# Attention and two feed-forward layers on one core: a PSUM tile for each bank, float64 weights converted two pieces at a time, the end of attention planned with the first weights

## The chip, the cores and the metric

The kernel runs on one core of a Trainium2 chip. The metric is the device time of one execution in microseconds. TensorE (PE), VectorE (DVE), ScalarE (ACT), GpSimd (POOL) and SyncE (SP) each work through a queue of their own in order; SP issues nearly all transfers. Matrix products accumulate in PSUM, which has eight banks of 512 fp32 columns in each of 128 partitions.

## The reference

```python
def _attn_ref(q, k, v, cap):                       # 2 x 12 heads x 448 x 64
    scores = cap * np.tanh(scale * np.matmul(q, k.transpose(0, 1, 3, 2)) / cap)
    scores = scores - np.max(scores, axis=-1, keepdims=True)
    attn = np.exp(scores)
    attn = attn / (np.sum(attn, axis=-1, keepdims=True) + 1e-09)
    return np.matmul(attn, v)
...
x = attn_out.transpose(0, 2, 1, 3).reshape(896, 768)
h = x @ moe_w_in                                   # 768 x 2048, float64
x = np.where(h > 0.0, h, np.exp(np.minimum(h, 0.0)) - 1.0) @ moe_w_out
h = np.maximum(x @ moe2_w_in, 0.0)
return (h * h @ moe2_w_out).astype(np.float32)
```

The four weight matrices arrive as float64 and are turned into fp32 on the core. Each fp32 operand is split in a high and a low part (`xh`, `xl`), and a product is three matmuls: high by high, high by low, low by high.

## The kernel before, in words

Attention goes through twelve pairs of heads, `pairs[n]`, in an order written out by hand. The end of a pair is a chain: `pv_out` copies the result out of PSUM (`pvs`, ACT), a transfer brings the row of sums (`den`), DVE takes the reciprocal (`rd`, in `norm`), two more transfers spread it over the partitions (`far`, `bc`), and `norm_x` multiplies (`xn`) and splits into `xh` and `xl`. The first two column blocks of layer 1 (`First`, accumulated in `begun`) are multiplied while the last pairs finish; their sixth input chunk, `kc` = 5 with batch 1, needs the last pair.

From there on a planner (`Plan`) takes tasks with costs and the keys that they read and write, walks through them in time, and so sets each engine's order; PE's order is that of the tasks. In the planner's keys each PSUM bank is separate. The weights come in 93 pieces of 512 columns. A piece is loaded into one of five `raw` buffers, converted by three steps on ACT and two on DVE into one of three `f` buffers (L777 to L785), for a Strassen quad widened by three subtractions (L798, L804), and split into two of the `og` tiles (L811, L812, L817). Four or five pieces can wait there or be in use.

Each layer has four phases of 512 hidden columns. A phase computes two quads, (phase, 0) and (phase, 1), of 256 hidden columns each, and multiplies them with the output weights. A plain quad is 72 matmuls; a Strassen quad has seven terms, in the order 1, 5, 6, 2, 7, 3, 4, of nine matmuls each, 63. Terms 1, 6, 7, 4 run up in bank X, which is copied out in between (L926 on ACT or L927 on DVE), term 2 in bank Z, to which DVE adds an earlier copy (`plus`, L933), terms 5 and 3 in bank Y. The Strassen terms need sums of the inputs (`sums`, tiles `yh` and `yl`). In layer 1 the quads after the first two are Strassen, in layer 2 those after the first, 13 in all. The output of layer 2 is made token tile by token tile, in one bank each (`out2_side`, `out2_main`, matmuls at L1050), and DVE adds a finished bank to the result (L1086; in the first phase a copy, by ACT at L1080 or DVE).

PSUM is four tiles of two banks each:

```python
units = begun + [pacc.tile([P, 2, W], F32, name=f"acc{i}") for i in range(2)]
...
ux, uy = units[2 * s], units[2 * s + 1]
X, Z, Y = ((ux[:, 0, :S], ("bank", 2 * s, 0)), (ux[:, 1, :S], ("bank", 2 * s, 1)),
           (uy[:, 0, :S], ("bank", 2 * s + 1, 0)))
```

The framework that turns the program into instructions sets the semaphore waits from the tiles that an instruction touches and the order of the program.

Of the kernel before, what the change touches and what calls it, by code (L numbers as in the profile page):

```python
# [29 lines left out]
def attention_moe_kernel(  # L30
# [238 lines left out]
    def split_p(n, i, copy=nc.vector.tensor_copy):  # L269
        if n < 0:  # L270
            return
# [6 lines left out]
        copy(h, e)  # L278
        nc.vector.tensor_tensor(l, e, h.bitcast(F32), op=ALU.subtract)
# [27 lines left out]
    def pv_out(n, copy=nc.scalar.copy):  # L307
        if n < 0:
            return
        pvs = ap_.tile([P, 2, S], F32, name="pvs", tag="pvs", bufs=3)  # L310
        copy(pvs, st["po", n][:, :, :S])
        st["pvs", n] = pvs
        den = ap_.tile([D, 2 * S // D], F32, name="den", tag="den")
        nc.sync.dma_start(den, pvs[D:D + 1].rearrange("p h s -> p (h s)"))
        st["den", n] = den

    def norm(n):


        if n < 0:  # L320
            return
        den = st["den", n]
        rd = ap_.tile([D, 2 * S // D], F32, name="rd", tag="rd")
        nc.vector.reciprocal(rd, den)
        far = dp.tile([D, 2 * S // D], F32, name="far", tag="far")
        nc.sync.dma_start(far, rd)
        bc = ap_.tile([D, 2, S], F32, name="bc", tag="bc")
        flat = far.rearrange("p s -> (p s)").unsqueeze(0)
        nc.sync.dma_start(bc.rearrange("p h s -> p (h s)"), flat.to_broadcast([D, 2 * S]))
        st["bc", n] = bc  # L330
# [22 lines left out]
    class First:  # L353


        def __init__(self):
            self.loaded, self.done = 0, 0
            self.alone = False
            self.rest = lambda: None
# [10 lines left out]
        def f(self, i):  # L370
            return fs[i % 2][:, :3]

        def load(self, dma=nc.sync.dma_start):
            i = self.loaded
            self.loaded += 1
            if i < self.COUNT:
                m, k = divmod(i, 2)
                dma(raws[i][:, :3], rows(w_in1, 3 * k, 3, m * P, P))

        def words(self, i):  # L380
            return words(raws[i][:, :3])
# [31 lines left out]
        def settle(self):  # L413
            last, self.rest = self.rest, lambda: None
            last()

# [66 lines left out]
    def dve(n, fast=False):  # L483
        return 0.12 + n / (1920 if fast else 960)

    def act(n):
        return 0.2 + n / 1200
# [3 lines left out]
    class Plan:  # L491
# [7 lines left out]
        def add(self, options, reads=(), writes=(), lag=None):  # L499
# [16 lines left out]
            self.tasks.append((options, before, self.LAG if lag is None else lag))  # L516

        def run(self, free):
# [66 lines left out]
            for _, _, _, _, fn in self.order:  # L585
                fn()

# [5 lines left out]
    def early(i):  # L593
        for to, src in in_loads(w_in1, 1, i):
            nc.sync.dma_start(to(raws[RAWS[i]]), src)
# [4 lines left out]
    with tc.manual_schedule():  # L600
# [36 lines left out]
        for n in range(np_):  # L637
# [27 lines left out]
            elif n < 4 + EARLY and n > 3:  # L665
                early(n - 4)
# [25 lines left out]
        late_kc = 2 * (KC - 1)  # L692
        norm(np_ - 2)
        emit(first.advance())
        split_p(np_ - 1, 1)
        mm_in(0, begun[0], kb[6::2])
        pv(np_ - 1, 1)
        pv_out(np_ - 1)
        emit(norm_x(np_ - 3))
        emit(first.advance())  # L700
        mm_in(0, begun[0], kb[1:7:2])
        x, x_high, x_low = norm_x(np_ - 2)
        x()
        first.settle()
        norm(np_ - 1)
        mm_in(1, begun[1], kb[0::2])
        x_high()
        x_low()
        mm_in(0, begun[0], kb[7:late_kc:2])
        mm_in(1, begun[1], kb[1:late_kc:2])  # L710
        x, x_high, x_low = norm_x(np_ - 1, nc.scalar.copy)
        x()
        x_high()
        x_low()
        attn.close()
        pacc = ctx.enter_context(tc.tile_pool(name="pacc", bufs=1, space=PSUM))
        gp = ctx.enter_context(tc.tile_pool(name="gp", bufs=1))
        units = begun + [pacc.tile([P, 2, W], F32, name=f"acc{i}") for i in range(2)]
        raws.append(gp.tile([P, 4, P], I64, name="raw4"))
        fs.append(gp.tile([P, 8, P], F32, name="f2"))  # L720
        groups += [gp.tile([P, 7, P], F32R, name=f"og{i}") for i in range(4, 8)]
        yh, yl = (gp.tile([P, 4, KH, S], F32R, name=x) for x in ("yh", "yl"))
        gh, gl = (gp.tile([P, PF, NT], F32R, name=x) for x in ("gh", "gl"))
        eps = [gp.tile([P, 2, S], F32, name=f"ep{i}") for i in range(4)]
        yp = gp.tile([P, KC, NT], F32, name="yp")
        yt = yp.rearrange("p c n -> p (c n)").rearrange("p (t d) -> p t d", d=DM)

        plan = Plan()
        add = plan.add
        counts = {"piece": 0, "ep": 0, "set": 1}  # L730
        slots = list(OGS)
# [13 lines left out]
        def piece(loads, full):  # L745

            i = counts["piece"]
            counts["piece"] += 1
            r, k, s = RAWS[i % 5], FS[i % 3], slots.pop(0)
            slots.append(s)  # L750
            raw, f = raws[r], fs[k]
            kr, ka, kx = ("raw", r), ("f", k), ("fx", k)
# [3 lines left out]
            else:  # L756
                h, l = (z[:, 1, :KH].rearrange("p c n -> p (c n)")[:, :7 * P].rearrange(
                    "p (a n) -> p a n", n=P) for z in (xh, xl))
                kh, kl = ([(("x", kc, 1), z) for kc in range(KH)] for z in "hl")

            def load():
                for to, src in loads:
                    nc.sync.dma_start(to(raw), src)

            if i >= EARLY:
                add((SP, 2.9, load), writes=[kr], lag=1.5)
            lo, hi = words(raw)
            a = f[:, :4]
            if i % VMOD in VSET:
# [406 lines left out]
```

## Time and profile before

| what | value |
|---|---|
| median of 3 runs | 626.05 us (625.68 to 626.82) |
| the profiled execution | 627.81 us |
| span of its profile | 626.0 us |
| mean granted TensorE clock | 0.986 |
| PE, DVE, ACT busy | 93%, 81%, 68% of the span |
| matmuls | 2945 |

Rows of the trace give times in us from the start of the span. A row of the timeline has the start, the duration, the engine, the line, the operation, what it writes and reads, and in brackets how long the engine was idle before it and what ended that. A matmul's end is modelled; consecutive matmuls overlap, so the pace is read from start to start.

### The profile page before, as it was taken

The numbers are of one execution on the slowest core, as the hardware profiler recorded it, in microseconds if no ns is written. First come the engines' busy times: TensorE is split into PE (matmuls) and PEld (weight loads), VectorE is DVE, ScalarE is ACT, GpSimd is POOL, SyncE is SP. The second block draws the span as 40 slices with busy tenths as digits, with TensorE's granted clock in tenths as the row PEclk, the third lists the DMA queues.
The fourth block names the chain that finished last, engine by engine and source line by source line (L and its number), as shares of the span: only waits on it lengthen the run. The fifth ranks groups of instructions, "written<-read, shape, count | busy, mean of one in ns | idle before, by whom it ended". The sixth has DMA issues, their size and how long they took to land.

```text
span 626.0 us, 8153 instructions
## 1 busy us (share of the span) xinstructions
PE 579.6 (93%) x2945; PEld 496.0 (79%) x2945; DVE 504.6 (81%) x818; ACT 424.7 (68%) x575; POOL 17.2 (3%) x30
## 2 busy tenths in 40 slices
PE   8899999989999999999999997998999999999996
PEld 8676777768997799889888996886788778877884
DVE  4599999869898889789878899786688868877823
ACT  5799899638997896787668857774675467546400
POOL 3111011000000000000000000000000000000000
PEclk9899999997999999999999998999999999999999
DMA  5646641117433344224414423143234323321013
GB/s 126 159 99 153 146 106 46 35 55 228 126 112 102 99 138 142 93 102 134 135 34 147 124 68 100 45 160 101 69 111 129 97 68 129 121 88 34 1 60 117
DMA packets 70280, 64.71 MB, mean 103 GB/s; under 512 B 38240, under 2 KB 52960, under 8 KB 70240
## 3 DMA queue, kind: packets, MB, share of 16 engines
q1 hardware_dynamic: 68736, 63.57, 34.4%
q10 hardware_dynamic: 1504, 0.62, 0.4%
q8 instruction: 23, 0.38, 0.3%
q14 instruction: 17, 0.14, 0.1%
HBM read 61.34 MB, written 2.80 MB: 102 GB/s over the span
## 4 chain that ended last, share of the span: by engine, by line
PE 80%; DVE 7%; DMA 4%; ACT 4%; issue 2%; SPq 2%; POOL 0%; ACTq 0%; DVEq 0%; POOLq 0%
PE acc L1050 19%; PE acc L474 18%; PE acc L476 17%; PE acc L475 17%; PE po L302 6%; PE sc L250 3%; DMA qz<-in_q_dram 2%; DVE yp L1086 1%; DVE acc L933 1%; PE pt L183 1%; ACT e L259 1%; DVE ep L927 1%; SPq L133 1%; DVE xn L342 1%; DMA raw<-in_moe_w_in_dram 1%
## 5 line engine op out<-in xcount | busy, mean ns | idle before, releaser
L1050 PE MATMUL acc<-og,gh 128*128 128x512 f32 (+1 forms) x350 | 87.9, 342 | 8.2 <-DVE yp L1086 5.5
L779 ACT ACTIVATE f<-raw 128x512 f16<-128x512 f32 x93 | 73.3, 788 | 21.1 <-DVE f L785 15.5
L811 ACT CAST og<-f 128x512 fp32r<-128x512 f32 (+1 forms) x57 | 43.1, 763 | 60.1 <-DVE f L804 25.1
L1050 PEld LDWEIGHTS acc<-og,gh 128*128 128x128 f32 x350 | 59.7, 190 | 18.7 <-DVE yp L1086 8.0
L474 PE MATMUL acc<-xh,og 128*128 128x448 f32 x165 | 62.8, 381 | 11.2 <-DVE ep L927 4.3
L781 ACT ACTIVATE f<-raw 128x512 uint16<-128x512 uint8 x93 | 72.2, 778 | 0.0
L817 DVE TENSOR_TENSOR og<-f,og 128x512 fp32r<-128x512 f32 (+1 forms) x76 | 64.3, 850 | 5.2 <-ACT og L811 3.9
L785 DVE SCALAR_TENSOR_TENSOR f<-f 128x512 uint32<-128x512 uint32 x93 | 63.9, 688 | 5.0 <-ACT f L781 1.7
L777 ACT ACTIVATE f<-raw 128x512 f32<-128x512 f32 x93 | 60.5, 658 | 2.9 <-DVE og L817 2.4
L475 PE MATMUL acc<-xl,og 128*128 128x448 f32 x165 | 61.5, 373 | 0.2 <-DVE xl L349 0.2
L476 PE MATMUL acc<-xh,og 128*128 128x448 f32 x165 | 61.4, 372 | 0.0
L1050 PE MATMUL acc<-og,gl 128*128 128x512 f32 (+1 forms) x175 | 59.2, 338 | 0.0
L475 PE MATMUL acc<-gl,og 128*128 128x448 f32 x160 | 58.6, 366 | 0.0
L476 PE MATMUL acc<-gh,og 128*128 128x448 f32 x160 | 58.6, 366 | 0.0
L474 PE MATMUL acc<-gh,og 128*128 128x448 f32 x160 | 58.6, 366 | 0.0
L474 PE MATMUL acc<-yh,og 128*128 128x448 f32 x124 | 47.4, 382 | 9.1 <-DVE acc L933 7.3
L475 PE MATMUL acc<-yl,og 128*128 128x448 f32 x124 | 46.3, 373 | 2.1 <-DVE yl L862 2.1
L259 ACT ACTIVATE e<-sc,tsc 128x896 f32<-128x896 f32 (+1 forms) x48 | 43.4, 911 | 4.7 <-PE sc L250 4.7
L474 PEld LDWEIGHTS acc<-xh,og 128*128 128x128 f32 x165 | 31.6, 192 | 18.7 <-DVE ep L927 6.6
L476 PE MATMUL acc<-yh,og 128*128 128x448 f32 x124 | 46.2, 372 | 0.0
L1086 DVE TENSOR_TENSOR yp<-yp,acc 128x512 f32<-128x512 f32 (+1 forms) x33 | 21.6, 661 | 27.5 <-PE acc L1050 27.2
L783 DVE TENSOR_SCALAR f<-f 128x512 f32<-128x512 f32 x93 | 39.1, 421 | 2.8 <-ACT f L777 2.2
(145 smaller groups left out, 1280.4 us busy)
## 6 DMA issues: line engine op xcount, KB each, us to landing
raw<-in_moe_w_in_dram SPq DMA_DIRECT2D x45, 512.0 KB, 4.0
raw<-in_moe_w_out_dram SPq DMA_DIRECT2D x48, 256.0 KB, 3.9
raw<-in_moe_w_out_dram SPq DMA_DIRECT2D x24, 512.0 KB, 3.7
bc<-far SPq DMA_DIRECT2D x12, 224.0 KB, 3.3
k<-in_k_dram SPq DMA_DIRECT2D x15, 128.0 KB, 2.9
q<-in_q_dram SPq DMA_DIRECT2D x15, 128.0 KB, 2.8
v<-in_v_dram SPq DMA_DIRECT2D x15, 128.0 KB, 3.4
out_dram<-yp SPq DMA_DIRECT2D x7, 256.0 KB, 2.0
```

Of the source, the lines that this page charges most:

```text
L259: nc.scalar.activation(st["e", n][:, 2 * c:2 * c + w], st["sc", n, c][:, :w, :S], AF.Tanh, scale=tsc)
L474: nc.tensor.matmul(acc, w[0], x[0], start=first, stop=False, skip_group_check=True)
L475: nc.tensor.matmul(acc, w[0], x[1], start=False, stop=False, skip_group_check=True)
L476: nc.tensor.matmul(acc, w[1], x[0], start=False, stop=last, skip_group_check=True)
L777: add((ACT, act(512), lambda: nc.scalar.activation(a, hi.bitcast(F32), AF.Abs, scale=2.0 ** 16)), [kr], [ka])
L779: add((ACT, act(512), lambda: nc.scalar.activation(top, hi.bitcast(F32), AF.Copy, scale=2.0 ** -100)), [kr], [kx])
L781: add((ACT, act(512), lambda: nc.scalar.activation(bottom, last, AF.Copy, scale=1 / 32, bias=-31 / 64)), [kr], [kx])
L783: add((DVE, dve(512, True), lambda: nc.vector.tensor_scalar(a, a, 2.0, 2.0 ** 16 * CLAMP, op0=ALU.max, op1=ALU.min)), [ka], [ka])
L785: add((DVE, dve(512), lambda: nc.vector.scalar_tensor_tensor(out=b, in0=b, scalar=3, in1=q.bitcast(U32), op0=ALU.logical_shift_left, op1=A ...
L811: (ACT, act(n * P), lambda: nc.scalar.copy(h[:, :n], src)),
L817: (DVE, dve(n * P), lambda: nc.vector.tensor_tensor(l[:, :n], src, h[:, :n].bitcast(F32), op=ALU.subtract)),
L1050: nc.tensor.matmul(acc, x[:, f, g], w, start=a, stop=z, skip_group_check=True)
```

## The change

PSUM after attention becomes eight tiles of one bank each (`bank(i)`), four in the place of `psc` and four in the place of `ps1`. An instruction that read or wrote two banks becomes two (`halves` in `evac`, `out_add`). In a Strassen quad the copy of X after term 7 and the add that followed become one add. Weights are loaded and converted as couples of two pieces, in two `raw` and two `f` buffers of two pieces each; the split into `og` remains by piece. The quad (1, 0) of layer 1 and (0, 1) of layer 2 become plain. The end of attention, the last parts of `First` and the first third of the quad (0, 1) are put into a plan of their own, run before the SBUF of attention is given back. Couple 1 is loaded into the `raw` buffer that `First` gives back, ahead of the last `den` in SP's queue.

```diff
-    raws = [wp.tile([P, 4, P], I64, name=f"raw{i}") for i in range(4)]
-    fs = [wp.tile([P, 8, P], F32, name=f"f{i}") for i in range(2)]
+    raws = [wp.tile([P, 2, 4, P], I64, name=f"raw{i}") for i in range(2)]
+    fs = [wp.tile([P, 2, 8, P], F32, name="f0")]
...
+        def bank(i, n=S):
+
+            if banks[i] is None:
+                old, side, four = (scp, "left", range(4)) if i < 4 else (ps1x, "right", range(4, 8))
+                old.close()
+                pool = ctx.enter_context(tc.tile_pool(name=f"bank{side}", bufs=1, space=PSUM, side=side))
+                for k in four:
+                    banks[k] = pool.tile([P, W], F32, name=f"acc{k}")
+            return banks[i][:, :n]
...
+            raw, f = raws[k % 2], fs[(k + 1) % 2]
+            n = len(couples[k])
...
+            e = 512 * n
+            b = a.bitcast(U32)
+            add((ACT, act(e) + 0.04 * n, lambda: nc.scalar.activation(a, hi, AF.Abs, scale=2.0 ** 16)), kr, ka)
+            add((ACT, act(e) + 0.17 * n, lambda: nc.scalar.activation(
+                top, hi, AF.Copy, scale=2.0 ** -100)), kr, kx)
+            add((ACT, act(e) + 0.17 * n, lambda: nc.scalar.activation(
+                bottom, byte, AF.Copy, scale=1 / 32, bias=-31 / 64)), kr, kx)
+            add((DVE, dve(e, True), lambda: nc.vector.tensor_scalar(
+                a, a, 2.0, 2.0 ** 16 * CLAMP, op0=ALU.max, op1=ALU.min)), ka, ka)
+            add((DVE, dve(e), lambda: nc.vector.scalar_tensor_tensor(
+                out=b, in0=b, scalar=3, in1=q.bitcast(U32),
+                op0=ALU.logical_shift_left, op1=ALU.bitwise_or)), ka + kx, ka)
...
-                add((ACT, act(n), lambda: nc.scalar.activation(t, h, AF.Relu, scale=-1.0)), hk, tk)
+                    halves(ACT, act(S), lambda a, h: nc.scalar.activation(a, h, AF.Relu, scale=-1.0))
...
-            ux, uy = units[2 * s], units[2 * s + 1]
-            X, Z, Y = ((ux[:, 0, :S], ("bank", 2 * s, 0)), (ux[:, 1, :S], ("bank", 2 * s, 1)),
-                       (uy[:, 0, :S], ("bank", 2 * s + 1, 0)))
+            X, Z, Y = range(4 * s, 4 * s + 3)
...
-                7: (X, 3, lambda j: y(2, j), False, (c, ck, 0)),
+                7: (X, 3, lambda j: y(2, j), False, None),
...
+                if p == 7:
+                    plus(part(c, ck, 0), in_x, part(d, dk, 1))
...
-                        (DVE, dve(NT), lambda to=to, u=u: nc.vector.tensor_tensor(to, to, u, op=ALU.add)),
-                        keys + [("yp", m)], [("yp", m)],
-                    )
+                for b in range(B):
+                    at = 4 * s + 2 * i + b
+                    out_add(ph, gpart(yp, m, b), lambda at=at: bank(at), [("bank", at)], [("yp", m, b)], S)
...
+        end, before = np_ - 1, np_ - 2
+        norm_tasks(before)
+        first_tasks(2)
...
+        norm_x_tasks(before)
+        norm_tasks(end)
+        for kc in range(KC):
+            begun_product(1, kc, 0)
...
+        norm_x_tasks(end)
+        s1 = next_set()
+        made = [piece() for _ in range(KH - 1)]
+        plain_products(s1, range(1), made)
+        to_fp32()
+        free = plan.run({PE: 3.1, DVE: 2.1, ACT: 0.3, SP: 0.0})
+        attn.close()
```

How PE's rows change inside the Strassen quad (1, 1) of layer 1, with the semaphores that a row waits for, named by the engine that raises them. Before, the tile of banks X and Z is `acc`, that of bank Y too; the rows are the end of term 2 (`xh`, `xl`, into Z) and the start of term 7 (`yh`, `yl`, into X), with `og_77` to `og_80` and a part of `xh` as the weights:

```order
L476 MATMUL acc<-xh,og_78 128x448
L474 MATMUL acc<-xh 128x448
L475 MATMUL acc<-xl,xh 128x448
L476 MATMUL acc<-xh,xl 128x448
L474 MATMUL acc<-xh,og_79 128x448 [waits Activation_49]
L475 MATMUL acc<-xl,og_79 128x448
L476 MATMUL acc<-xh,og_80 128x448
L474 MATMUL acc<-yh,og_77 128x448
L475 MATMUL acc<-yl,og_77 128x448
L476 MATMUL acc<-yh,og_78 128x448
L474 MATMUL acc<-yh,xh 128x448 [waits DVE_49]
```

In the changed kernel bank X is `acc_1614`, Z `acc_1615` and Y `acc_1616`. The same place, from the last matmul of term 6 over term 2 to the first of term 7:

```order
L475 MATMUL acc_1614<-yh,og_75 128x448
L473 MATMUL acc_1615<-xh,og_1346 128x448
L474 MATMUL acc_1615<-xl,og_1346 128x448
L475 MATMUL acc_1615<-xh,og_1347 128x448
L473 MATMUL acc_1615<-xh,og_1348 128x448
L474 MATMUL acc_1615<-xl,og_1348 128x448
L475 MATMUL acc_1615<-xh,og_1349 128x448
L473 MATMUL acc_1615<-xh,og_74 128x448
L474 MATMUL acc_1615<-xl,og_74 128x448
L475 MATMUL acc_1615<-xh,og_75 128x448
L473 MATMUL acc_1614<-yh,og_1346 128x448 [waits DVE_49]
```

The wait inside term 2 is gone, and the wait at the start of term 7 is on another instruction: the copy of X that follows term 6, nine matmuls earlier.

ACT's rows at the end of attention, before; `e` is the last pair's scores, `f_75` and `f_76` belong to `First`, `f_1462` is the first converted piece of the planned weights, `raw_71` its float64 source:

```order
L259 ACTIVATE e<-sc,tsc 128x448 [waits PE_49]
L267 ACTIVATE e<-e,capt 128x1344 [waits Activation_49]
L409 CAST og_79<-f_75 128x384 [waits DVE_49]
L311 COPY pvs<-po 128x896 [waits DMAHW1_49,PE_49]
L409 CAST og_80<-f_76 128x384 [waits DVE_49]
L348 CAST xh<-xn 128x448 [waits DVE_49]
L779 ACTIVATE f_1462<-raw_71 128x512 [waits DMAHW3_49,DMAHW4_49,DMAHW2_49,DMAHW5_49,DMAHW1_49,DMAHW6_49,DMAHW0_49,DMAHW7_49,DVE_49,Pool_49]
L777 ACTIVATE f_1462<-raw_71 128x512
L781 ACTIVATE f_1462<-raw_71 128x512
L779 ACTIVATE f_75<-raw_72 128x512
```

And now, where `f_1345` and `raw_71` are the first couple, `f_73` and `raw_72` first the last parts of `First` and then the second couple:

```order
L261 ACTIVATE e<-sc,tsc 128x448 [waits PE_49]
L269 ACTIVATE e<-e,capt 128x1344 [waits Activation_49]
L806 ACTIVATE f_1345<-raw_71 128x2x512 [waits DMAHW5_49,DMAHW3_49,DMAHW6_49,DMAHW1_49,DMAHW7_49,DMAHW0_49,Pool_49]
L805 ACTIVATE f_1345<-raw_71 128x2x512
L808 ACTIVATE f_1345<-raw_71 128x2x512
L420 CAST og_76<-f_73 128x384 [waits DVE_49]
L322 COPY pvs<-po 128x896 [waits DMAHW1_49,PE_49]
L420 CAST og_77<-f_73 128x384 [waits DVE_49]
L806 ACTIVATE f_73<-raw_72 128x2x512 [waits DMAHW4_49,DMAHW3_49,DMAHW2_49]
L805 ACTIVATE f_73<-raw_72 128x2x512 [waits DVE_49]
L844 CAST og_1346<-f_1345 128x512 [waits DVE_49]
```

The split of the last pair's `xh` has left ACT's queue for DVE's, and the conversions of the first couple stand ahead of the copy of the last pair's `pvs`.

PE's rows where the last pair is first needed, before: six products of `kc` = 5 into `begun` (`acc`), and then the plain quad (0, 1) in `acc_1459`:

```order
L474 MATMUL acc<-xh,og_80 128x448
L475 MATMUL acc<-xl,og_80 128x448
L476 MATMUL acc<-xh,og_80 128x448
L474 MATMUL acc<-xh,og_78 128x448 [waits Activation_49]
L475 MATMUL acc<-xl,og_78 128x448 [waits DVE_49]
L476 MATMUL acc<-xh,og_78 128x448
L474 MATMUL acc<-xh,og_80 128x448
L475 MATMUL acc<-xl,og_80 128x448
L476 MATMUL acc<-xh,og_80 128x448
L474 MATMUL acc_1459<-xh,og_1463 128x448 [waits DMAHW3_49,DMAHW4_49,DMAHW2_49,DMAHW5_49,DMAHW1_49,DMAHW6_49,DMAHW0_49,DMAHW7_49,PE_49,Activation_49]
L475 MATMUL acc_1459<-xl,og_1463 128x448
```

And now, where `acc_1474` to `acc_1477` are the four banks of the quad (0, 1):

```order
L475 MATMUL acc_1476<-xh,og_1347 128x448
L473 MATMUL acc_1477<-xh,og_1346 128x448
L474 MATMUL acc_1477<-xl,og_1346 128x448
L475 MATMUL acc_1477<-xh,og_1347 128x448
L473 MATMUL acc<-xh,og_75 128x448 [waits DVE_49]
L474 MATMUL acc<-xl,og_75 128x448 [waits DVE_49]
L475 MATMUL acc<-xh,og_75 128x448
L473 MATMUL acc<-xh,og_77 128x448
L474 MATMUL acc<-xl,og_77 128x448
L475 MATMUL acc<-xh,og_77 128x448
L473 MATMUL acc_1474<-xh,og_1348 128x448
```

The first third of that quad, 24 matmuls with `og_1346` and `og_1347`, stands ahead of the six products, its other two thirds behind them.

## Rows read from the trace of the kernel before

**Rows 1.** The page: busy us, share of the span, instructions of each engine.

```profile
PE 579.6 (93%) x2945; PEld 496.0 (79%) x2945; DVE 504.6 (81%) x818; ACT 424.7 (68%) x575; POOL 17.2 (3%) x30
```

**Rows 2.** Waits by cause: engine, line <- releaser: us in total, times, longest.

```profile
PE acc L474 <- DVE acc L933: 9.4, 13, 0.7
...
PE acc L474 <- DVE ep L927: 5.7, 8, 0.7
...
PE acc L474 <- ACT ep L926: 3.1, 5, 0.6
...
PE acc L1050 <- DVE yp L1086: 7.8, 10, 0.8
...
PE acc L1050 <- ACT yp L1080: 2.7, 4, 0.7
```

**Rows 3.** PE's timeline around attention's end: start, us, instruction, [idle before].

```profile
135.82 0.37 PE L476 MATMUL acc<-xh,og 128*128 128x448 f32 x1
...
138.52 0.37 PE L476 MATMUL acc<-xh,og 128*128 128x448 f32 x1
...
141.91 0.74 PE L474 MATMUL acc<-xh,og 128*128 128x448 f32 x1 [3.02 <-ACT og L811]
...
147.82 0.37 PE L474 MATMUL acc<-xh,og 128*128 128x448 f32 x1
...
159.37 0.37 PE L474 MATMUL acc<-gh,xh 128*128 128x448 f32 x1
```

**Rows 4.** PE's timeline inside the Strassen quad (1, 1) of layer 1.

```profile
209.94 0.37 PE L476 MATMUL acc<-xh,xl 128*128 128x448 f32 x1
...
210.93 0.47 PE L474 MATMUL acc<-xh,og 128*128 128x448 f32 x1 [0.62 <-ACT ep L926]
...
211.24 0.36 PE L475 MATMUL acc<-xl,og 128*128 128x448 f32 x1
...
212.04 0.37 PE L476 MATMUL acc<-yh,og 128*128 128x448 f32 x1
...
213.14 0.47 PE L474 MATMUL acc<-yh,xh 128*128 128x448 f32 x1 [0.73 <-DVE acc L933]
```

**Rows 5.** PE's timeline in the last phase of layer 2's output.

```profile
614.54 0.61 PE L1050 MATMUL acc<-og,gh 128*128 128x512 f32 x2
...
614.99 0.39 PE L1050 MATMUL acc<-og,gl 128*128 128x512 f32 x1
...
616.16 0.73 PE L1050 MATMUL acc<-og,gh 128*128 128x512 f32 x2 [0.78 <-DVE yp L1086]
```

**Rows 6.** PE's timeline in the Strassen quad (0, 1) of layer 2.

```profile
382.32 0.37 PE L476 MATMUL acc<-yh,xl 128*128 128x448 f32 x1
...
387.03 0.74 PE L475 MATMUL acc<-yl,og 128*128 128x448 f32 x1 [2.07 <-DVE yl L862]
...
396.14 0.37 PE L476 MATMUL acc<-yh,xl 128*128 128x448 f32 x1
```

**Rows 7.** Two stretches: length, busy us of PE, PEld, DVE, ACT, POOL, PEclk, DMA.

```profile
145.00:200.00 55.00, 54.38 (x262) 49.90 (x261) 51.08 (x87) 48.87 (x72) 0.00 (x0) 0.98 0.45 138
...
380.00:400.00 20.00, 14.77 (x54) 11.77 (x54) 16.46 (x25) 12.32 (x20) 0.00 (x0) 0.83 0.24 77
```

**Rows 8.** DVE and ACT at attention's end, timeline.

```profile
129.80 0.23 DVE L324 RECIPROCAL rd<-den 64x14 f32<-64x14 f32 x1
...
135.04 1.25 DVE L342 TENSOR_TENSOR xn<-pvs,bc 64x448 f32<-64x448 f32 x2 [4.11 <-DMA bc<-far]
...
136.33 0.56 ACT L348 CAST xh<-xn 128x448 fp32r<-128x448 f32 x1 [7.64 <-DVE xn L342]
```

**Rows 9.** Groups by line: xcount | busy, mean ns of one | idle before.

```profile
L779 ACT ACTIVATE f<-raw 128x512 f16<-128x512 f32 x93 | 73.3, 788 | 21.1 <-DVE f L785 15.5 <-DVE og L817 3.3 <-DVE xl L817 1.4
...
L785 DVE SCALAR_TENSOR_TENSOR f<-f 128x512 uint32<-128x512 uint32 x93 | 63.9, 688 | 5.0 <-ACT f L781 1.7
```

**Rows 10.** The page's DMA issues: xcount, KB each, median us to landing.

```profile
raw<-in_moe_w_in_dram SPq DMA_DIRECT2D x45, 512.0 KB, 4.0
```

More of the change, by code (lines that the diff above doesn't have):

```diff
@@ L1 @@
-import itertools
 import math
@@ L709, in attention_moe_kernel @@
[L709 to L726, printed above, removed]
+        early.close()
@@ L756, in piece @@
             else:
[L757 to L768, printed above, removed]
@@ L915, in strassen_quad, with plus @@
             }
-            for p, js in order:
-                (acc, bank), o, other, first, copy = terms[p]
-                for j in js:
+            def plus(to, a, b):
+                get = lambda z: z[1]() if callable(z[1]) else z[1]
+                add((DVE, dve(S), lambda: nc.vector.tensor_tensor(get(to), get(a), get(b), op=ALU.add)),
+                    [a[0], b[0]], [to[0]])
+            in_x, in_z, in_y = held([X, Z, Y])
+            part = lambda t, tk, i: ((tk, i), t[:, i])
+            for p in (1, 5, 6, 2, 7, 3, 4):
+                at, o, other, first, copy = terms[p]
+                for j in range(KH):
                     h, l, pk = parts[j]
                     z, zk = other(j)
-                    product(acc, bank, pk + zk, (h[:, o], l[:, o]), z, first and j == 0, j == KH - 1)
-                if copy and js[-1] == KH - 1:
+                    product(at, pk + zk, (h[:, o], l[:, o]), z, first and j == 0, j == KH - 1)
+                if p == 7:
+                    plus(part(c, ck, 0), in_x, part(d, dk, 1))
+                if copy:
                     t, tk, i = copy
@@ new lines, in first_tasks @@
+        def first_tasks(i):
+            sgn, lw, high, rest = first.end(i)
+            clp, shf = first.begin(i)
+            k = ("of", i)
+            if i == 3:
+                add((DVE, 0.36, clp), [k], [k])
+                add((DVE, 0.36, shf), [k], [k])
+            add((DVE, 0.54, sgn), [k, ("raw", 1, i - 2)], [k])
+            add((DVE, 0.54, lw), [k, ("raw", 1, i - 2)], [k])
+            add((ACT, 0.52, high), [k], [("first", i), k])
+            add((DVE, 0.55, rest), [k], [("first", i), ("f", 1, i - 2), ("fx", 1, i - 2)])
@@ new lines, in attention_moe_kernel @@
+        end, before = np_ - 1, np_ - 2
+        norm_tasks(before)
+        first_tasks(2)
+        h, l = split_p_steps(end, 1)
+        add((DVE, 0.62, h), [], [("p", 1)])
+        add((DVE, 1.09, l), [], [("p", 1)])
+        for kc in range(KH, KC):
+            begun_product(0, kc, 0)
+        add((PE, 2.3, lambda: pv(end, 1)), [("p", 1)], [("po", 0)])
+        copy, den = pv_out_steps(end)
+        add((ACT, 0.91, copy), [("po", 0)], [("pvs", end)])
+        add((SP, 0.49, den), [("pvs", end)], [("den", end)], 1.9)
@@ L1141, in attention_moe_kernel @@
             counts["set"] += 1
-        plan.run({PE: 0.0, DVE: 0.0, ACT: 0.0, SP: 0.0})
+        plan.run(free)
 _INS = ["q", "k", "v", "cap", "moe_w_in", "moe_w_out", "moe2_w_in", "moe2_w_out"]
```

542 lines of the change are left out of this document (291 added, 251 removed).

## Prediction

> **What bounds the kernel now.** I read the page first: PE is busy 93% of the span, DVE 81% [rows 1]. The reader is to see that PE is the engine that the others feed, and that 46.4 us (626.0 less 579.6) is all the idle time this column leaves. Then the waits: three kinds of PE wait come back at a fixed count, 13 for Strassen's `plus` into Z (L933), 8 + 5 for the copy of X (L927 on DVE, L926 on ACT), 10 + 4 for the adds that empty the banks of the second layer's output (L1086, L1080) [rows 2]. Thirteen is the number of Strassen quads. Then the timeline at each kind, where I measured from the start of one matmul to the start of the next, against the pace of undisturbed ones: 57 matmuls of 448 columns from 147.82 to 159.37 take 11.55 us, 0.203 us each [rows 3].
>
> A Strassen quad [rows 4]: 209.94 to 210.93 is 0.99 us where 0.20 is due, so 0.79 lost; the next start is 0.31 later, 0.11 more. 212.04 to 213.14 loses 0.90, and I take the same 0.11 after it. Term 2 writes bank Z and waits for a copy out of bank X; term 7 writes X and waits for an add in Z. X and Z are halves of one tile `units[2s]`: neither wait is between users of one bank. One quad loses 1.91 us; where DVE makes the copy the idle time is 0.71 instead of 0.62 [rows 2], 0.1 more.
>
> The second layer's output [rows 5]: two 512-column matmuls start between 614.54 and 614.99, 0.23 each; 614.99 to 616.16 loses 0.94, with the restart 1.05; where ACT empties the bank, 0.1 less by the idle times of [rows 2]. The wait comes each time that token tile t ends in one half of a unit and t + 1 goes on in the other.
>
> **The first weighing.** By the busy column nothing beyond 46.4 us can be removed; by start to start the four places of this sum alone lose 54.9 us. The modelled end of a matmul lies 0.37 us after its start at a pace of 0.203 [rows 4], so each wait hides its first 0.17 us in "busy". The Trainium skill (Perfetto Trace Analysis, Identifying the Most-Contended Engine) says that matmul busy time is a poor measure of the room left because matmuls are pipelined, and names the busy share of the weight loads instead; here that is 79% against 93% [rows 1], so the trace agrees. By the busy column the best possible would be 627.8 - 46.4 + 3.6 = 585 us; I go by the starts.
>
> **The change part by part.** Times are of the profiled execution, 627.81 us with a span of 626.0, which is 1.76 above the median of the runs (626.05).
>
> 1. One PSUM tile per bank. Gone: 13 x 1.91 + 8 x 0.1 = 25.6 us in the quads, 10 x 1.05 + 4 x 0.95 = 14.3 us in the output. The order of the changed kernel shows that term 2 has no wait left, and that term 7 waits for the copy of its own bank, with the nine matmuls of term 2 (1.8 us) in between. Price of it: evacuations of two banks are now two instructions, on ACT and DVE beside PE: nothing on the path.
>
> 2. The quad (0, 1) of the second layer and (1, 0) of the first are plain: 72 matmul instructions instead of 63 each, 18 x 0.203 = 3.65 us more. The former buys this: after 382.32 PE waits for the y tiles twice (2.07 us for `yl` the second time), and the matmuls behind that run slower; 27 starts from 382.32 to 396.14 take 13.82 us where 5.47 are due, 8.35 lost, of which 0.9 is a copy's wait already counted: 7.45 us [rows 6]. The granted clock over 380 to 400 is 0.83 [rows 7]. The y sums then have both plain quads to hide behind, 144 x 0.203 = 29 us; without that cover the 7.45 us are back.
>
> 3. The end of attention. 22 starts from 135.82 to 147.82 take 12.00 us, 4.46 are due, 7.54 lost [rows 3]: 3.19 in the gap before 141.91, 2.9 after it at half pace, the rest before. The chain: ACT sits at L348 for 7.64 us, waiting for `xn`, which waits 4.11 for the `bc` transfer; all the weight conversions stand behind it in its queue [rows 8]. Now ACT converts the first couple while it would wait, and PE has 24 matmuls of the plain quad (4.9 us) between the other products and the last six. PE reaches these six at 136.03 + 4.9 = 140.9. What is late next: `recip` of the last pair, which started at 129.80 [rows 8], now stands on DVE behind the two 1024-wide steps of the first couple (at most 1.38 each by [rows 9]) and behind the split of the last pair but one, which stood behind it (I estimate 0.8): 129.8 + 2.8 + 0.8 = 133.4. Behind it follow the same steps as before, 129.80 to the end of `xh` at 136.9, 7.1 us: 140.5, and 0.6 for `xl`. So a wait of about 0.5 us is left; bounds 0 and 4 (2 us of delay, since SP issues three weight loads ahead of `den` and they share the transfer engines, and as much again at the lower clock). Gain 7.5, cost 0.5.
>
> 4. Conversions of 1024 columns. 92 of the 93 pieces go in 46 pairs. A 1024-wide step costs between one and two of today's: 0.79 to 1.58 us on ACT, 0.69 to 1.38 on DVE [rows 9]; from the fixed part that a second instruction no longer pays I take about 1.35 and 1.2. Some 30 us of ACT and 20 of DVE are saved, none of it on PE's path: taken at nothing. It matters from 145 to 200, where DVE is busy 51.1 and ACT 48.9 of 55 us while PE hardly waits [rows 7]; with the waits gone PE asks sooner. I take 1 us, bounds 0 and 5.
>
> 5. `c0` is now one add on DVE straight from bank X, before a copy on either engine and an add in SBUF. PE needs X again in term 4, one term (1.82 us) later. From [rows 4] the shortest way from the last matmul through such an add to the next is 1.10 us start to start, so DVE may be 0.92 late. One wide step in front (up to 1.38) costs up to 0.5. I take 0.1 x 11 quads = 1.0; bounds 0 and 11 x 1.4 (two steps in front) = 15.
>
> Sum: 627.81 - 25.6 - 14.3 - 7.45 - 7.54 + 3.65 + 0.5 + 1 + 1 = 579.1 us; less 1.76, **577.3**. With nothing lost newly 574.8.
>
> **The rivals.**
> *ACT and DVE cannot keep up* (steps 4, 5): PE asks 8% faster, and the wider steps block a queue longer. For it: the stretch from 145 in [rows 7]. Against: in both engines the work shrinks about as much as the span. 6 to 15 us of new waits: 583 to 592.
> *A new gap at the end of attention*, because den, far and bc are later than I put them. From rows: the gap of 3.19 us before 141.91 was followed by matmuls at 0.37 us each, the 1.2 GHz level, 15 starts to 147.82 that cost 2.9 more [rows 3]; so a gap of 3 costs 6: 583. The Trainium skill (TensorE: Matmul & The Clock Gate, What's actually happening) has it that half rate is the state of rest and that activity lifts it, so an idle PE pays again after a gap; both gaps here agree.
> *The waits stay*: if the pairing of banks were not the tile's doing, step 1 gives nothing: 577.3 + 39.9 = 617. Against it: the order no longer has these waits.
> *Slower.* One mechanism: the raw buffers are two couples, and a load is issued only when the three ACT steps on the couple before it in the same buffer are done. A couple lasts PE 42 x 0.203 = 8.5 us in a quad, so a buffer has 17.0 us to turn round. Two loads at 4.0 [rows 10] one after the other and three ACT steps at 1.58 are 12.7. To eat the net 49 us, each of 46 couples must be 1.1 us late, a turn of 19.2 us: it decides from 6.5 us of queueing per couple. Then 627 or more.
>
> **How the numbers follow.** Forecast (572.5 to 582) 0.63; engines late 0.18; gap at the end of attention 0.12; waits stay, in whole or part, 0.05; slower 0.02. The range 572.5 to 592 holds the first three, less some of their tails: about 0.88; its lower end is 574.8 less 2.3 for waits around 119 to 125 that the new order might also mend. A measurement of this kernel tells 0.2% (1.25 us) from no change: faster 0.97, within it 0.01, slower 0.02.
>
> **What would show it.** No wait of PE on L926, L927, L933's or the adds' successors at 0.6 to 0.8 us; PE idle below 20 us in all; no stretch after 116 with a granted clock below 0.95; 18 more matmuls; six products of the last pair within 1 us of the plain ones before them; conversion steps of 1024 at 1.1 to 1.4 us on ACT. It would be wrong if PE waits for `og` halves or for term 4's bank in every quad, if a gap above 2 us stands near 141, or if a copy in another bank still stops a matmul.

## The result, and the profile after

The changed kernel takes 582.25 us (median of 4 runs, 580.89 to 583.57), against 626.43 for the kernel before beside it: 0.929 of its time, 95% interval 0.9255 to 0.9325. The prediction was 577.3, with a range of 572.5 to 592.0. The profiled execution took 583.39 us; all rows of "after" below are from it.

The page's busy times, which answer to [rows 1]:

```profile
span 581.6 us, 7854 instructions
PE 569.8 (98%) x2963; PEld 497.8 (86%) x2963; DVE 485.9 (84%) x690; ACT 403.7 (69%) x439; POOL 17.0 (3%) x30
```

PE is idle 11.8 us of 581.6, and the 18 more matmuls are there (2945 before). The waits of PE by what ended them (total us, times, longest):

```profile
PE pt L185 <- DMA q<-in_q_dram: 3.3, 7, 0.8
PE sc L213 <- POOL ident masks.py:199: 1.6, 1, 1.6
...
```

Every wait in this list belongs to attention; the three kinds of [rows 2] are gone, and after 130 us no wait of PE is left. The Strassen quad (1, 1) in PE's timeline, end of term 6 (`yh`), term 2 (`xh`), start of term 7 (`yh`), where [rows 4] lost 1.91 us:

```profile
204.46 0.37 PE L475 MATMUL acc<-yh,og 128*128 128x448 f32 x1
204.67 0.36 PE L473 MATMUL acc<-xh,og 128*128 128x448 f32 x1
204.87 0.37 PE L474 MATMUL acc<-xl,og 128*128 128x448 f32 x1
...
206.29 0.37 PE L475 MATMUL acc<-xh,og 128*128 128x448 f32 x1
206.49 0.36 PE L473 MATMUL acc<-yh,og 128*128 128x448 f32 x1
206.70 0.37 PE L474 MATMUL acc<-yl,og 128*128 128x448 f32 x1
```

Every start is 0.20 or 0.21 after the one ahead of it. The end of attention, answering to [rows 3, 8]: the six products of the last pair begin at 143.84. On DVE `recip`, the last `xn` and its split are the rows to find: `xh` is done at 143.34 and `xl` at 144.00, just in time for the first product with `xl` at 144.06:

```profile
143.63 0.37 PE L475 MATMUL acc<-xh,og 128*128 128x448 f32 x1
143.84 0.36 PE L473 MATMUL acc<-xh,og 128*128 128x448 f32 x1
144.06 0.47 PE L474 MATMUL acc<-xl,og 128*128 128x448 f32 x1
144.37 0.36 PE L475 MATMUL acc<-xh,og 128*128 128x448 f32 x1
```
```profile
134.06 0.69 DVE L810 TENSOR_SCALAR f<-f 128x1024 f32<-128x1024 f32 x1
134.78 1.23 DVE L812 SCALAR_TENSOR_TENSOR f<-f 128x1024 uint32<-128x1024 uint32 x1
135.92 0.23 DVE L337 RECIPROCAL rd<-den 64x14 f32<-64x14 f32 x1
...
141.66 0.62 DVE L354 TENSOR_TENSOR xn<-pvs,bc 64x448 f32<-64x448 f32 x1 [1.58 <-DMA bc<-far]
...
142.95 0.39 DVE L360 CAST xh<-xn 128x448 fp32r<-128x448 f32 x1
143.37 0.63 DVE L361 TENSOR_TENSOR xl<-xn,xh 128x448 fp32r<-128x448 f32 x1
```

The whole loss there is 0.1 us, in one start of 0.31. The stretches of [rows 7] have no gap and no lowered clock (columns: stretch, its length, busy us and instructions of PE, weight loads, DVE, ACT and POOL, granted clock, share of the transfer engines, GB/s):

```profile
145.00:200.00 55.00, 55.00 (x271) 50.47 (x270) 51.74 (x78) 46.64 (x58) 0.00 (x0) 1.00 0.37 115
380.00:400.00 20.00, 20.00 (x130) 18.31 (x129) 18.75 (x28) 19.68 (x23) 0.00 (x0) 1.00 0.31 106
```

So the four terms of gain came in full, and of the three new costs (0.5, 1 and 1 us) 0.1 is left. By the sum that would be 576.7 us in the profiled execution; it took 583.39. Where PE never waits, 6.7 us more can only lie ahead of the stretch, or in the pace.

**Ahead of it.** The last pair's `pv` stops for `exp` at 121.02, in the kernel before at 118.13. The other eleven profiles, of the kernel before and of the experiments below, have this stop between 117.17 and 119.71, five of them of programs that are the changed kernel's up to there (117.97 to 119.71). The 2.9 us belong to this execution, not to the change, and the trace shows where they arise. PE waits for transfers of `q`, and the transposition of `qz` that starts at 74.96 in the kernel before starts at 76.42: 1.46 us later. Behind these waits the granted clock falls for a while from 2.4 to 1.2 GHz, and the next 50 matmuls take 9.97 us (to 86.39) instead of 8.49: 1.48 us more. The stretch from 77 to 82, first of the kernel before, then of the changed one (length, busy us of PE, granted clock, share of the transfer engines, GB/s):

```profile
77.00:82.00 5.00, 5.00 (x28) 1.00 0.56 141
```
```profile
77.00:82.00 5.00, 5.00 (x24) 0.66 0.48 118
```

A stretch at the lower clock stands near 20 us in every profile but that of e6_apart. A later one in attention is in three of the other profiles alone (e6_apart, 0.72 over 74 to 80; e7_copy and e10_aligned128, 0.66 over 57 to 62); e3_two_bank, e4_halves and e5_strassen, the same program up to there, have none.

**The pace.** An output block of layer 1 is 144 matmuls of 448 columns, from the first that moves `gh` to the first that moves `xh` again:

```profile
212.02 0.37 PE L473 MATMUL acc<-gh,xh 128*128 128x448 f32 x1
...
241.78 0.36 PE L473 MATMUL acc<-xh,og 128*128 128x448 f32 x1
...
396.98 0.63 PE L1080 MATMUL acc<-og,gh 128*128 128x512 f32 x2
...
399.78 0.40 PE L1080 MATMUL acc<-og,gh 128*128 128x512 f32 x1
```

29.76 / 144 = 0.2067 us each, at a granted clock of 1.00, where the prediction counted 0.203 for all. The 12 matmuls of 512 columns from 396.98 to 399.78 take 0.2333 each. Over all matmuls after 128 us, by the records' starts: products that move `x` 203.0 ns, products that move `y` or `g` 205.9 (203.5 in the kernel before), 512-column products with `g` as the weights 233.3 (227.8). What separates them is where the tiles lie. The changed kernel puts `yh`, `yl`, `gh`, `gl` in a pool on the right side of SBUF, which fills from the top; in the built program `yh` begins at byte 121824 of a partition, 32 past a multiple of 64, and the other three likewise. In the kernel before it began at 121536, a multiple of 64, as `xh` and `xl` do in both.

### The profile page after: what moved, and what is told of

Read it like the earlier page. It is cut to its first block, busy times and chain, and to the rows that moved or that the text cites. A ratio compares the mean times of both kernels' runs of the same rounds, so it can differ in the third digit from the quotient of the medians.

```text
span 581.6 us, 7854 instructions
## 1 busy us (share of the span) xinstructions
PE 569.8 (98%) x2963; PEld 497.8 (86%) x2963; DVE 485.9 (84%) x690; ACT 403.7 (69%) x439; POOL 17.0 (3%) x30
## 4 chain that ended last, share of the span: by engine, by line
PE 88%; DMA 4%; SPq 3%; ACT 1%; DVE 1%; issue 1%; POOL 0%; ACTq 0%; DVEq 0%; POOLq 0%
PE acc L1080 20%; PE acc L474 19%; PE acc L473 19%; PE acc L475 19%; PE po L308 7%; PE sc L252 3%; DMA qz<-in_q_dram 2%; DMA v<-in_v_dram 1%; PE pt L185 1%; SPq L135 1%; ACT e L261 1%; DMA raw<-in_moe_w_in_dram 1%; SPq L150 1%; DMA q<-in_q_dram 0%; DVE pl L284 0%
## 5 line engine op out<-in xcount | busy, mean ns | idle before, releaser
L475 PE MATMUL acc<-xh,og 128*128 128x448 f32 x201 | 73.5, 366 | 0.0
L473 PE MATMUL acc<-xh,og 128*128 128x448 f32 x201 | 73.5, 366 | 0.0
L474 PE MATMUL acc<-xl,og 128*128 128x448 f32 x201 | 73.5, 366 | 0.0
L806 ACT ACTIVATE f<-raw 128x1024 f16<-128x1024 f32 (+1 forms) x47 | 64.3, 1368 | 6.2 <-DMA raw<-in_moe_w_out_dram 3.9
L808 ACT ACTIVATE f<-raw 128x1024 uint16<-128x1024 uint8 (+1 forms) x47 | 64.2, 1366 | 0.0
L1109 DVE TENSOR_TENSOR yp<-yp,acc 128x448 f32<-128x448 f32 (+2 forms) x69 | 43.6, 639 | 20.5 <-PE acc L1080 14.8
L812 DVE SCALAR_TENSOR_TENSOR f<-f 128x1024 uint32<-128x1024 uint32 (+1 forms) x47 | 56.8, 1209 | 1.2
L805 ACT ACTIVATE f<-raw 128x1024 f32<-128x1024 f32 (+1 forms) x47 | 52.6, 1120 | 3.5 <-DVE og L850 3.4
L473 PEld LDWEIGHTS acc<-xh,og 128*128 128x128 f32 x201 | 37.7, 188 | 3.4 <-ACT e L261 0.2
L475 PEld LDWEIGHTS acc<-xh,og 128*128 128x128 f32 x201 | 37.7, 188 | 3.4 <-DVE og L850 0.2
L474 PEld LDWEIGHTS acc<-xl,og 128*128 128x128 f32 x201 | 37.8, 188 | 3.3 <-DVE xl L361 0.2
L473 PE MATMUL acc<-yh,og 128*128 128x448 f32 x108 | 39.9, 369 | 0.0
```

The source lines that it names most:

```text
L473: nc.tensor.matmul(acc, w[0], x[0], start=first, stop=False, skip_group_check=True)
L474: nc.tensor.matmul(acc, w[0], x[1], start=False, stop=False, skip_group_check=True)
L475: nc.tensor.matmul(acc, w[1], x[0], start=False, stop=last, skip_group_check=True)
L805: add((ACT, act(e) + 0.04 * n, lambda: nc.scalar.activation(a, hi, AF.Abs, scale=2.0 ** 16)), kr, ka)
L806: add((ACT, act(e) + 0.17 * n, lambda: nc.scalar.activation(top, hi, AF.Copy, scale=2.0 ** -100)), kr, kx)
L808: add((ACT, act(e) + 0.17 * n, lambda: nc.scalar.activation(bottom, byte, AF.Copy, scale=1 / 32, bias=-31 / 64)), kr, kx)
```

## The experiments

### Where the tiles lie

```diff
+    edge = ctx.enter_context(tc.tile_pool(name="edge", bufs=1, side="right"))
+    nc.vector.memset(edge.tile([P, 8], F32, name="edge"), 0.0)
     one = attn.enter_context(tc.tile_pool(name="one", bufs=1, side="right"))
```

> The changed kernel with 32 unused bytes ahead of the tiles on the right side of SBUF, so that yh, yl, gh, gl (and the attention tiles there) begin at a multiple of 64 bytes as they do in the kernel before; in the changed kernel they begin 32 bytes past one. Theory A (the place of these tiles sets the pace): products that move y or g go from 205 to 207 ns start to start back to the 202.7 of those that move x: 972 x 3.5 ns = 3.4 us, and the 512-column products with g as weights from about 234 to 227 ns, 336 x 6 = 2.0, the 256-column ones give back up to 1.0. So 582.25 - 4.4 = 577.9, 576.5 to 579.5. Theory B (the pace is set by how PE last started again after a wait, whatever the address): 582.25 within 2.5 either way, and products that move y or g stay above 205 ns where those that move x are at 202.7. The start of the last pv at 121.0 shows beside it whether the 2.9 us that attention is longer go with the addresses (A': back to 118.1) or not.

578.1 us (577.22 to 580.87), ratio 0.9211 [0.9186, 0.9237], below the changed kernel's interval. The same two places:

```profile
209.74 0.36 PE L475 MATMUL acc<-gh,xh 128*128 128x448 f32 x1
...
238.92 0.36 PE L475 MATMUL acc<-xh,og 128*128 128x448 f32 x1
...
393.23 0.62 PE L1082 MATMUL acc<-og,gh 128*128 128x512 f32 x2
...
395.95 0.39 PE L1082 MATMUL acc<-og,gh 128*128 128x512 f32 x1
```

29.18 / 144 = 0.2026, and 2.72 / 12 = 0.2267. Products that move `y` or `g` are at 202.9 ns on the mean; the 256-column ones went the other way, 118.3 to 119.9. The reverse was done to the kernel before:

```diff
         groups += [gp.tile([P, 7, P], F32R, name=f"og{i}") for i in range(4, 8)]
+        nc.vector.memset(gp.tile([P, 8], F32, name="edge"), 0.0)
```

> The kernel before with 32 unused bytes ahead of yh, yl, gh, gl and the tiles after them, attention untouched. Theory A: products that move y or g slow down from 202.6 to about 206 ns and the 512-column ones from 227 to about 234: 3.4 + 2.0 us (some of it hidden by waits), 629 to 632 against 626.4. Theory B: 626.4 within 1.5.

631.1 us (629.09 to 633.58) against 627.81 beside it, ratio 1.005 [1.0032, 1.0068]: 3.3 us slower, with 205.6 and 233.3 ns in the trace. Theory A holds in both directions. The tiles behind these four (`ep`, `yp`) moved along each time; that the products that move `x` kept 203 ns speaks for the operands, but the runs don't part the two. A third place was tried:

```diff
-    nc.vector.memset(edge.tile([P, 8], F32, name="edge"), 0.0)
+    nc.vector.memset(edge.tile([P, 24], F32, name="edge"), 0.0)
```

> The kernel e1_aligned with 96 instead of 32 unused bytes, so that yh, yl, gh, gl begin at a multiple of 128 bytes; in e1_aligned and in the kernel before they begin 64 past one. If a multiple of 64 is all that counts: paces as in e1_aligned (202.9 ns for products that move y or g, 227.0 for the 512-column ones) and 578.1 within 1.5. If a larger step counts: shorter paces still, 2 us or more less.

577.7 us (577.34 to 579.04), the time of e1_aligned, but not its paces: products that move `y` or `g` are at 202.1 ns, those that move `x` at 205.5, and the 512-column ones at 229.0. The total agrees with "a multiple of 64 counts"; the paces say that this isn't the whole rule.

### The four gains, undone one by one

**One tile per bank (step 1).**

```diff
-                for k in four:
-                    banks[k] = pool.tile([P, W], F32, name=f"acc{k}")
+                for k in four[::2]:
+                    two = pool.tile([P, 2, W], F32, name=f"acc{k}")
+                    banks[k], banks[k + 1] = two[:, 0], two[:, 1]
```

> The changed kernel with PSUM in tiles of two banks again (banks 2i and 2i+1 are halves of one tile), everything else as changed. My theory (step 1: the waits come from two users of one tile): 11 Strassen quads x 1.91 plus 14.3 us in the second layer's output come back: 21.0 + 14.3 + 0.8 = 36, so about 618 (614 to 622), with PE waits of 0.6 to 0.8 us in terms 2 and 7. Rival (the waits are real uses of a bank and went with the plain quads and the merged add): 582 to 586.

617.08 us (616.51 to 619.19): 34.8 us more. The waits are back, by kind and in the timeline:

```profile
PE acc L473 <- DVE acc L972: 6.5, 9, 0.7
PE acc L473 <- DVE ep L990: 5.0, 7, 0.7
PE acc L1081 <- DVE yp L1110: 3.9, 5, 0.8
...
PE acc L473 <- ACT ep L989: 2.5, 4, 0.6
...
570.26 0.36 PE L475 MATMUL acc<-xh,og 128*128 128x448 f32 x1
571.25 0.47 PE L473 MATMUL acc<-xh,og 128*128 128x448 f32 x1 [0.62 <-ACT ep L989]
```

Inside term 2, 570.26 to 571.25 is 0.99 us where 0.20 is due, as in [rows 4]. The tiling of PSUM alone is worth 35 of the 44 us.

**The plain quad of layer 2 (step 2).**

```diff
-                if ph:
+                if ph + q:
                     strassen_quad(next_set(), ph * QP + q, "relu2")
...
-            if ph == 0:
-                for j in range(KH):
-                    yp_sums(j)
-                slots.insert(0, 4)
+                    for j in range(KH):
+                        yp_sums(j)
+                    slots.insert(0, 4)
```

> The changed kernel with the quad (0, 1) of layer 2 as a Strassen quad again, its sums planned ahead of it as before. My theory (step 2: the plain quad gives the y sums the time they need): 9 matmuls fewer, -1.83 us, and PE waits for yh and yl after the first quad of layer 2 with a lower clock behind it, +7.45: 582.25 + 5.6 = 587.9 (585.5 to 590). Rival (the sums were late because ACT and DVE were held up by what the rest of the change mended; they now come in time): 580.4, no PE wait above 0.5 us between 365 and 390 and a granted clock of 1.00 there.

589.21 us (588.49 to 590.67), 7.0 more. Waits, and the stretch with its clock:

```profile
PE acc L473 <- ACT yh L905: 4.2, 1, 4.2
...
PE acc L474 <- DVE yl L911: 0.7, 1, 0.7
...
365.00:385.00 20.00, 14.51 (x51) 11.74 (x50) 17.22 (x23) 15.76 (x20) 0.00 (x0) 0.74 0.32 106
...
367.44 0.37 PE L475 MATMUL acc<-yh,xl 128*128 128x448 f32 x1
...
381.88 0.37 PE L473 MATMUL acc<-xh,og 128*128 128x448 f32 x1
```

The sums are late by themselves, not because of what else was mended: with 9 matmuls fewer the stretch costs 7.0 + 1.83 = 8.8 us by the medians where step 2 said 7.45. In the timeline it is 10.0: 22 starts from 367.44 to 381.88 take 14.44 us where 4.46 are due, a copy's wait among them that step 2 had left out.

**The common plan at the end of attention (step 3).**

```diff
-        s1 = next_set()
-        made = [piece() for _ in range(KH - 1)]
-        plain_products(s1, range(1), made)
-        to_fp32()
         free = plan.run({PE: 3.1, DVE: 2.1, ACT: 0.3, SP: 0.0})
...
+        s1 = next_set()
+        made = [piece() for _ in range(KH - 1)]
+        plain_products(s1, range(1), made)
+        to_fp32()
         for ph in range(PH):
```

> The changed kernel with the first third of the quad (0, 1) and the conversions of the first couples taken out of the plan of attention's end and put behind it, where the SBUF of attention has been given back. My theory (step 3: these products are what PE has to do while xh and xl of the last pair are made): a gap of about 3 us before the six last products of the begun blocks, near 139 to 142, and half pace behind it: 582.25 + 7.5 less the 1 to 2 us that the earlier conversion alone may give, 587 to 591. Rival (the gap went because of the order of the rest, den, far and bc sooner): 582 to 584.

592.59 us (591.11 to 592.72), 10.3 more, above my range of 587 to 591. PE's rows that waited:

```profile
141.19 0.74 PE L473 MATMUL acc<-xh,og 128*128 128x448 f32 x1 [3.19 <-DVE xh L360]
147.85 0.74 PE L473 MATMUL acc<-xh,og 128*128 128x448 f32 x1 [3.77 <-ACT og L844]
```

The first gap stands before the six products of the last pair and waits for `xh`. The kernel before had this wait too, but a short one, ahead of the gap of [rows 3]:

```profile
136.94 0.48 PE L474 MATMUL acc<-xh,og 128*128 128x448 f32 x1 [0.76 <-ACT xh L348]
```

The second gap is the counterpart of the one at 141.91 in [rows 3] (3.02 us idle there): it waits for the first `og` of the quad (0, 1), whose conversions stand behind the end of attention again. So both waits of the kernel before are back, and longer. Both gaps end at half pace, rows of 0.74 and 0.57 us instead of 0.36; the granted clock is 0.51 from 141 to 151, nearly all of it at 1.2 GHz. Together, 15 starts from 137.62 to 150.94 take 13.32 us where 3.05 are due: 10.3 lost, the whole difference between the medians.

### The three new costs

**Width (step 4).** Each of the five steps of a couple was put out as two of 512 columns:

```diff
-            e = 512 * n
+            def steps(a, q, hi, byte, top, bottom, kr, ka, kx):
+                e, n = 512, 1
...
+            for i in range(n):
+                cut = lambda t: t if n == 1 else t[:, i]
+                a1, q1, hi1, byte1, top1, bottom1 = (cut(t) for t in (a, q, hi, byte, top, bottom))
+                steps(a1, q1, hi1, byte1, top1, bottom1, *([x[i]] for x in (kr, ka, kx)))
```

> The changed kernel with each conversion step of a couple as two instructions of 512 columns; loads, buffers and order rules as changed. My theory (step 4: the wide steps save busy time off PE's path): ACT busier by about 46 x 3 x 0.25 = 34 us and DVE by about 46 x 2 x 0.17 = 16, the time within 1.5 us of 582.25, and no PE wait above 0.3 us after 130. Rival (ACT and DVE are at their limit once PE's waits are gone): PE waits between 145 and 200 and in the Strassen quads, 585 to 597.

581.12 us (580.42 to 584.99), ratio 0.9269 [0.9242, 0.9297]: no difference from 0.929, and no PE wait longer than 0.34 us after 130. The steps by group (count, busy us, mean ns), first of the changed kernel, then of this one:

```profile
L806 ACT ACTIVATE f<-raw 128x1024 f16<-128x1024 f32 x46 | 63.5, 1381 | 6.2 <-DMA raw<-in_moe_w_out_dram 3.9 <-DVE og L850 1.3 <-DMA raw<-in_moe_w_in_dram 0.8
L812 DVE SCALAR_TENSOR_TENSOR f<-f 128x1024 uint32<-128x1024 uint32 x46 | 56.1, 1220 | 1.2
```
```profile
L807 ACT ACTIVATE f<-raw 128x512 f16<-128x512 f32 x93 | 71.5, 784 | 8.0 <-DVE og L855 3.7 <-DMA raw<-in_moe_w_in_dram 1.7 <-DVE xl L855 1.3
L813 DVE SCALAR_TENSOR_TENSOR f<-f 128x512 uint32<-128x512 uint32 x93 | 62.9, 687 | 3.3 <-ACT f L809 1.1
```

1.38 us against twice 0.78 on ACT, 1.22 against twice 0.69 on DVE: durations as estimated (1.35 and 1.2). ACT as a whole grew from 403.7 to 416.5 us, DVE from 485.9 to 490.2, less than the 34 and 16 expected of it, and none of it reaches PE.

**One add instead of copy and add (step 5).**

```diff
-                7: (X, 3, lambda j: y(2, j), False, None),
+                7: (X, 3, lambda j: y(2, j), False, (c, ck, 0)),
...
-                if p == 7:
-                    plus(part(c, ck, 0), in_x, part(d, dk, 1))
...
             plus(in_z, in_z, part(d, dk, 0))
+            plus(part(c, ck, 0), part(c, ck, 0), part(d, dk, 1))
```

> The changed kernel with step 5 alone undone: X after term 7 is copied by ACT or DVE and the sum made from the copy, 11 more instructions. The prediction priced the direct add at 1.0 us with a bound of 15 (DVE busy when term 7 ends). If that price is real: 581.2 or less. If term 4 never waits, as the trace of the changed kernel reads: 582.25 within 1 us, no wait in term 4 either way. A rise above 584 would say that the copies crowd ACT or DVE.

582.04 us (580.22 to 582.97): the same. PE loses nothing in term 4 in either form.

**The cover at attention's end.** In e1_aligned PE loses 1.2 us at the six last products, the wait that step 3 put at 0.5. More cover was tried:

```diff
-        plain_products(s1, range(1), made)
+        plain_products(s1, range(2), made)
...
-                plain_products(s1, range(1, KH), made + [piece()])
+                plain_products(s1, range(2, KH), made + [piece()])
```

> The kernel e1_aligned with two thirds of the quad (0, 1), 48 matmuls instead of 24, in the plan of attention's end. In e1_aligned PE lost 1.2 us at 140.85 to 142.35 before xh and xl of the last pair. If the cover is what was missing (step 3, whose sum left a wait of 0.5 us): no PE wait at that place and 578.1 - 1.2 = 577, with 4.9 us of room. If the conversions of the second piece are not ready that early: PE waits for og instead, a gap of 2 us or more near 136 to 142 with a lower clock behind it, 580 to 584.

583.44 us (581.2 to 585.9), slower than e1_aligned. Half of the first expectation came: the wait at 141 is gone. But PE now waits 12 us later, where the output block begins:

```profile
153.55 0.44 PE L475 MATMUL acc<-gh,og 128*128 128x448 f32 x1 [0.88 <-ACT gh L907]
155.00 0.47 PE L476 MATMUL acc<-gl,og 128*128 128x448 f32 x1 [1.01 <-DVE gl L913]
156.53 0.47 PE L476 MATMUL acc<-gl,og 128*128 128x448 f32 x1 [0.66 <-DVE gl L913]
```

The 24 matmuls that were moved forward had covered the making of `gh` and `gl`; these are now late by 2.55 us in all, 3.3 from start to start. Between the two profiled executions, 581.20 and 577.22 us, that is most of the difference: 3.3 us here, 1.4 in a stretch at the slower pace (the last section; 341 matmuls, 4 ns each) and 0.5 in attention, less the 1.2 at 141, make the 4.0. The medians lie 5.3 apart; the wide scatter of its runs stays unexplained.

**The plain quad (1, 0) of layer 1**, the other half of step 2's 18 matmuls:

```diff
-    PLAIN = 1, 0
+    PLAIN = 0, 1
...
-                if ph == PLAIN[0]:
-                    slots.insert(0, 4)
...
+                slots.insert(0, 4)
```

> The kernel e1_aligned with the quad (1, 0) of layer 1 as a Strassen quad again. If its y sums are ready in time, as in the kernel before: 9 matmuls fewer, 578.1 - 1.83 = 576.3, and no PE wait above 0.3 us in that quad. If the engines, freed of PE's waits, no longer have the sums ready (the reason for which a plain quad could stand there): PE waits of 1 us or more for yh or yl near 195 to 205 and 578 to 584.

579.32 us (577.9 to 579.53), not faster than 578.1 with 9 matmuls fewer. One wait, and the stretch behind it:

```profile
182.90 0.47 PE L477 MATMUL acc<-xh,og 128*128 128x448 f32 x1 [1.40 <-DVE og L852]
...
180.00:200.00 20.00, 18.34 (x80) 15.65 (x79) 18.17 (x26) 16.21 (x22) 0.00 (x0) 0.91 0.43 129
```

Not the sums are late, as I had expected, but the widened `og`: DVE was busy 19.2 of the 20 us before. From 181 to 189 PE loses 4.0 us, part of it at the lower clock (granted 0.91 over the stretch, 0.50 or 1.2 GHz from 185 to 188.2). That is more than the 1.83 that the quad saves.

## Why the prediction was right, and what it missed

*What bounds the kernel.* Right: by start to start there was more to remove than the idle column shows. The changed kernel took 583.39 us in its profile and 577.2 with the tiles aligned, below the 585 that the busy column allowed as the best case.

*Step 1*, 39.9 us: right. Undone in the changed kernel, where 11 of 13 Strassen quads are left, it gives back 34.8; the same prices make 11 x 1.91 + 0.8 + 14.3 = 36.1.

*Step 2*: right in kind, and too low: 8.8 us of waits and lowered clock by the medians, 10.0 by the timeline, for 7.45, at the price of 9 matmuls. The first layer's plain quad costs nothing measurable either, but for another reason than cover for the sums.

*Step 3*, 7.54 us: right. `recip` stands 135.92 - 121.02 = 14.9 us behind the last `pv`'s stop, before 129.80 - 118.13 = 11.7: 3.2 later, where the sum had 3.6. PE reaches the six products 22.8 us behind that stop; by the sum 140.9 - 118.1 = 22.8. The wait put at 0.5 us was 0.1 here and 1.2 in e1_aligned. Undone, it costs 10.3 us and not 7.54, because both waits are longer there than in the kernel before (from start to start 3.4 us for 0.9 and 4.1 for 3.2).

*Steps 4 and 5*, 1 us each: nothing, by the trace and by e4_halves and e7_copy. The rival that ACT and DVE cannot keep up had this for it: e8_aligned_strassen shows them over the edge with one Strassen quad more near 181.

*What failed* is the line that isn't a step: the sum kept the pace of [rows 3], 0.203 us, for every matmul, and has no term for the place that the move of pools to the right side gives the tiles. From the first planned product to the last matmul, the changed kernel takes 448.2 us (129.25 to 577.47) and e1_aligned 444.9 (126.46 to 571.33), of which 1.2 is its gap: 4.5 us for the pace. With it and the 2.9 us of this execution's attention the sum is 576.7 + 4.5 + 2.9 = 584.1 against 583.39. The aligned kernel's 578.1 is within a microsecond of the 577.3 forecast, and the fastest of both kernels and all variants but its twin e10_aligned128 (577.7).

*What was luck.* The 582.25 measured lies just above 582, where the forecast's own part of the range ended, in the part that was there for rivals that did not come. And two errors partly cancelled: 2.5 us of new costs were counted of which 0.1 came, and 4.5 us for the pace were not counted.

*The rivals.* The gap at attention's end, late engines, waits that stay and the raw buffers' turn did not come; PE has no wait for `og` after 130.

## What to carry to other kernels

Two users of different banks in one PSUM tile are put in order by the tile (34.8 us here, e3_two_bank), and the cost shows as a short wait at a fixed count; measure from start to start, not by the idle column. Work that is moved forward to fill a gap was covering something: look for what stands behind its old place. When a change moves a pool to another side or order, print where the operands of the matmuls begin, and compare the pace start to start of the same products.

## What the runs showed that I had not expected

At one granted clock (1.00) a 448-column product has two paces, about 202.7 and 206.7 ns, and a 512-column one with `g` as weights 227 and 233. The operands' place decides most of it: 32 bytes cost 4.2 us here and 3.3 us in the kernel before. The Trainium skill (SBUF — State Buffer, SBUF: two separate sides) says that transfers and engines use separate ports and that PE waits for nobody at its own. No run here tests that; e1_aligned shows only that the pace changed with the address while the work of the other engines stayed the same (DVE busy 485.4 us for 485.9, ACT 403.4 for 403.7). The Trainium skill (TensorE: Matmul & The Clock Gate, Wait — 56ns, not 53.3ns?) puts warm matmuls back to back N / 2.4 GHz plus about 2.5 ns apart, an estimate of 189 ns for 448 columns. Both paces here, where every matmul has a weight load of its own (2963 of each), are longer, and the measured ones decide.

The address is not all: in e9_two_thirds, with aligned tiles, one hiccup without a recorded wait changes the pace of everything behind it, `x` included:

```profile
310.40 0.37 PE L475 MATMUL acc<-xh,og 128*128 128x448 f32 x1
310.61 0.36 PE L476 MATMUL acc<-xl,og 128*128 128x448 f32 x1
310.86 0.47 PE L477 MATMUL acc<-xh,og 128*128 128x448 f32 x1
311.16 0.36 PE L475 MATMUL acc<-yh,og 128*128 128x448 f32 x1
```

0.25 and 0.30 us instead of 0.20, and then 206.7 ns until the width of the products changes at 381.8; ahead of it 202.7. The kernel before has such a stretch from 330 to 382. What sets this second state, and why the tiles of e10_aligned128 speed up `g` and slow down `x`, stays open.
